# The second MLP of a window attention and two-MLP kernel in three tiles of 768 tokens, each product 384 columns wide

## The chip, the cores and the metric

The program runs on one core of a Trainium2 chip. The metric is the device time of one execution in microseconds (us). Before the change three runs gave 883.8, 884.16 and 888.37 us, so the median is 884.16 us.

## The reference

Attention over a window of 64 positions (4 batches, 8 heads, 576 positions, head size 64) gives 2304 tokens of 512 features. Two MLPs follow, each 512 to 2048 to 512, all in float32:

```python
def _moe_ref(x, w_in, w_out):
    h = x @ w_in
    r = np.maximum(h, 0.0)
    g = r * r
    return (g @ w_out).astype(np.float32)

def _moe2_ref(x, w_in, w_out):
    h = x @ w_in
    g = np.maximum(h, 0.0) + np.log1p(np.exp(-np.abs(h)))
    return (g @ w_out).astype(np.float32)
...
    x = _moe_ref(x=x, **moe_kwargs)
    return _moe2_ref(x=x, **moe2_kwargs)
```

## The kernel before

**Products.** Every operand of an MLP is split into a high and a low part in a format that TensorE reads in one pass, and every product is three matmuls: high by high, low weights by high, high weights by low. The first product of an MLP (x by w_in) is done with seven products of half-size matrices in place of eight (the names A, B, C, T1, T2, T3, T4 stand for the seven). The sums of weights that this needs are prepared once (`add_weights`, `add_sums`) on VectorE (DVE) and ScalarE (ACT), stored to DRAM (`d_in`, `d_out`), and streamed back through the rings `ri` and `ro`; the sums of inputs are made by `add_mats` for each tile.

**Second MLP.** There are four tiles of 512 tokens and one of 256. A tile has eight blocks; `add_block` makes two chunks of 128 hidden features: 7 products of 6 matmuls with 256 columns. `PA` puts A and T2 side by side into one PSUM bank (`pa`), `PB` puts T3 and T1 into another (`pb`), ACT copies `pa` to `wk` (`EA`), DVE adds (`U2`, `UB`), then `PC` puts B and C into `pa`, `PD` puts T4 into `pb`, and DVE makes the two chunks (`CC`, `CD`). Four banks may hold such products (class `h2`), so two blocks can be in flight; the four others hold the sums of the second product (class `acc`). The tile of 256 tokens uses plain products (`l1_small`, 12 matmuls of 256 columns for a chunk). `add_smooth` then works on each chunk: ACT does Abs, Exp, +1 and Ln, DVE three operations; `add_split` gives `gh` (ACT) and `gl` (DVE). `add_l2` is the second product, job `K`: for each 128 tokens 3 matmuls of 512 columns into `acc`.

**Order.** A planner (class `Plan`) writes all engines' instructions out in one fixed order before launch: jobs wait for others, take slots of pools (`caps`), and run by a rank, which is a due time shifted by the table `SHIFT`. On the chip each engine runs its list strictly in that order. All DMAs are issued by SyncE (SP) in that order too. Preparing the second MLP's weights is interleaved with the first MLP and with the beginning of the second.

Names in instruction rows: `pa1_2_7` is the bank `pa` of the second MLP (1), tile 2, block 7; a number behind it is the buffer's. `gh1_3_2` is MLP 1, tile 3, chunk 2. `halvesw...` and `area` are buffers that were something else before.

Of the kernel before, what the change touches and what calls it, by code (L numbers as in the profile page):

```python
# [1387 lines left out]
```

## Time and profile before

| | us |
|---|---|
| median of three runs | 884.16 |
| the profiled execution | 885.8 |
| its span, first to last instruction | 884.0 |
| TensorE busy in the span | 861.9 |
| VectorE, ScalarE busy | 742.0, 597.2 |

The profiled execution took 1.8 us more than its span and lies 1.6 us above the median. TensorE's busy time is made from modelled ends of pipelined matmuls, so a busy TensorE may still be at less than its full rate; how far apart matmuls start tells the rate. The first MLP and attention take the span to about 500 us, the second MLP the rest; the two overlap around there.

### The profile page before, as it was taken

How to read it: one execution, taken by the hardware profiler on the slowest of the kernel's cores; microseconds unless marked ns; L12 is line 12 of the kernel's file. 1: busy time of each engine (PE TensorE's matmuls, PEld its weight loads, DVE VectorE, ACT ScalarE, POOL GpSimd, SP SyncE). 2: the span in 40 equal slices, each digit the busy share in tenths (PEclk: the TensorE clock that was granted, in tenths of full speed). 3: DMA queues.
4: the chain of work that ended last, by engine and by line, in shares of the span. 5: the costliest groups of instructions: out<-in, count | busy, mean ns of one | idle time of the engine just before them, and what ended most of it. 6: DMA issues, size and time to landing. Idle time of an engine off the chain costs nothing.

```text
span 884.0 us, 17073 instructions
## 1 busy us (share of the span) xinstructions
PE 861.9 (98%) x6220; PEld 783.1 (89%) x6220; DVE 742.0 (84%) x1404; ACT 597.2 (68%) x1266; POOL 3.6 (0%) x19
## 2 busy tenths in 40 slices
PE   7799999999999999999999999999999999999998
PEld 6599999999898889888899988888898989899897
DVE  6899999899999999599655999998779667877754
ACT  5777776577675776466445867868568667766765
POOL 1000000000000000000000000000000000000000
PEclk9899999999999999999999999999999999999999
DMA  9999987999999999999999999899936872788581
GB/s 203 315 288 364 308 307 235 297 322 301 338 288 371 278 315 333 312 350 315 331 346 349 342 340 367 327 324 335 325 124 198 298 256 66 265 276 276 181 294 49
DMA packets 169987, 254.35 MB, mean 288 GB/s; under 512 B 65584, under 2 KB 119856, under 8 KB 169904
## 3 DMA queue, kind: packets, MB, share of 16 engines
q1 hardware_dynamic: 169904, 253.27, 87.0%
q8 instruction: 49, 0.80, 0.4%
q14 instruction: 34, 0.28, 0.1%
HBM read 193.46 MB, written 59.77 MB: 286 GB/s over the span
## 4 chain that ended last, share of the span: by engine, by line
PE 76%; DVE 10%; SPq 5%; DMA 3%; ACT 3%; issue 2%; DVEq 0%; ACTq 0%
PE acc L826 38%; PE pa L998 5%; PE pa L1001 5%; PE pa L999 4%; PE pb L998 4%; PE pb L1001 3%; PE pb L999 3%; SPq L607 2%; PE h L799 2%; PE h L800 2%; PE h L802 2%; SPq L440 2%; PE sc L646 1%; PE po L709 1%; DVE gl L847 1%
## 5 line engine op out<-in xcount | busy, mean ns | idle before, releaser
L826 PE MATMUL acc<-ro,gh 128*128 128x512 f32 x576 | 178.8, 392 | 0.0
L826 PE MATMUL acc<-gh,ro 128*128 128x512 f32 x384 | 121.9, 399 | 0.5 <-ACT gh L844 0.5
L826 PEld LDWEIGHTS acc<-ro,gh 128*128 128x128 f32 x576 | 104.3, 189 | 18.6
L826 PE MATMUL acc<-ro,gl 128*128 128x512 f32 x288 | 112.1, 389 | 0.0
L1101 DVE SCALAR_TENSOR_TENSOR e<-u,e 128x512 f32<-128x512 f32 (+1 forms) x80 | 50.8, 635 | 56.4 <-ACT u L1095 56.3
L998 PE MATMUL pb<-xT,ri 128*128 128x256 f32 x336 | 89.0, 287 | 3.1 <-DVE wk L1030 1.8
L999 PE MATMUL pb<-xT,ri 128*128 128x256 f32 x336 | 87.8, 283 | 0.0
L826 PEld LDWEIGHTS acc<-gh,ro 128*128 128x128 f32 x384 | 69.7, 190 | 14.0 <-issue 0.7
L826 PE MATMUL acc<-gl,ro 128*128 128x512 f32 x192 | 75.6, 394 | 0.3 <-DVE gl L847 0.3
L844 ACT CAST gh<-l 128x512 fp32r<-128x512 f32 (+1 forms) x80 | 45.7, 572 | 44.3 <-DVE l L1105 29.5
L998 PEld LDWEIGHTS pb<-xT,ri 128*128 128x128 f32 x336 | 64.1, 191 | 5.7 <-DVE wk L1030 2.0
L1001 PE MATMUL pb<-xT,ri 128*128 128x256 f32 x336 | 67.8, 283 | 0.1
L826 PE MATMUL acc<-gh,w 128*128 128x384 f32 x256 | 66.0, 338 | 0.0
L999 PEld LDWEIGHTS pb<-xT,ri 128*128 128x128 f32 x336 | 64.3, 191 | 1.2
L826 PEld LDWEIGHTS acc<-ro,gl 128*128 128x128 f32 x288 | 54.1, 188 | 12.0 <-DVE gl L847 0.3
L847 DVE TENSOR_TENSOR gl<-l,gh 128x512 fp32r<-128x512 f32 (+1 forms) x80 | 50.4, 630 | 4.0 <-ACT gh L844 3.6
L1001 PEld LDWEIGHTS pb<-xT,ri 128*128 128x128 f32 x336 | 52.4, 192 | 0.3 <-DVE xT L971 0.3
L1105 DVE TENSOR_TENSOR l<-l,e 128x512 f32<-128x512 f32 (+1 forms) x80 | 50.6, 632 | 2.3
L1093 ACT ACTIVATE e<-c 128x512 f32<-128x512 f32 (+1 forms) x53 | 29.5, 556 | 31.2 <-DVE c L1035 11.9
L1096 ACT ACTIVATE l<-u 128x512 f32<-128x512 f32 (+1 forms) x80 | 47.2, 590 | 2.6
L1094 ACT ACTIVATE e<-e 128x512 f32<-128x512 f32 (+1 forms) x80 | 47.2, 590 | 2.5
L1095 ACT ACTIVATE u<-e 128x512 f32<-128x512 f32 (+1 forms) x80 | 47.2, 589 | 2.5
(226 smaller groups left out, 2298.6 us busy)
## 6 DMA issues: line engine op xcount, KB each, us to landing
ri<-di SPq DMA_DIRECT2D x154, 512.0 KB, 6.2
ro<-do SPq DMA_DIRECT2D x92, 512.0 KB, 6.2
ri<-di SPq DMA_DIRECT2D x46, 256.0 KB, 5.4
raw<-in_moe_w_in_dram SPq DMA_DIRECT2D x16, 512.0 KB, 8.8
raw<-in_moe_w_out_dram SPq DMA_DIRECT2D x16, 512.0 KB, 6.7
di<-w SPq DMA_DIRECT2D x32, 256.0 KB, 4.8
do<-w SPq DMA_DIRECT2D x16, 512.0 KB, 5.7
di<-osa SPq DMA_DIRECT2D x32, 256.0 KB, 5.4
```

The lines of the kernel that those rows point to most:

```text
L826: nc.tensor.matmul(o, lh, rh, start=st and i == 0, stop=sp and i == 2)
L844: nc.scalar.copy(out=place(j, f"gh{me}", [P, T], F32R), in_=live[src])
L847: nc.vector.tensor_tensor(out=place(j, f"gl{me}", [P, T], F32R), in0=live[src], in1=f32(live[f"gh{me}"]), op=ALU.subtract)
L998: nc.tensor.matmul(out, w[:, 0, c, :], x[:, 0, c, :], start=(c == 0), stop=False)
L999: nc.tensor.matmul(out, w[:, 1, c, :], x[:, 0, c, :], start=False, stop=False)
L1001: nc.tensor.matmul(out, w[:, 0, c, :], x[:, 1, c, :], start=False, stop=(c == 1))
L1093: nc.scalar.activation(out=e, in_=live[src], func=AF.Abs)
L1094: nc.scalar.activation(out=e, in_=e, func=AF.Exp, scale=-1.0)
L1095: nc.scalar.add(u, e, 1.0)
L1096: nc.scalar.activation(out=g, in_=u, func=AF.Ln)
L1101: nc.vector.scalar_tensor_tensor(out=e, in0=u, scalar=1.0, in1=e, op0=ALU.subtract, op1=ALU.subtract)
L1105: nc.vector.tensor_tensor(out=live[f"l{me}"], in0=live[f"l{me}"], in1=live[f"e{me}"], op=ALU.add)
```

## The change

The second MLP's tokens are cut into three tiles of 768, each half 384 tokens, so each of the seven products is 6 matmuls of 384 columns and fills a bank alone (384 of its 512 columns). `add_block2` takes the place of `add_block` there. A (`PA`) goes into a fresh bank `pa`, T2 (`PC`), T3 (`PE`) and T4 (`PF`) are added on to it in the bank; between them ACT copies the running sum out (`EA`, `EB`, `EC`, and `ED` on ACT or DVE). B (`PB`) fills `pb`, which DVE adds to the first copy (`CA`); T1 (`PD`) fills `pd`, DVE takes a sum (`CB`), C (`PG`) is added on, and DVE takes another (`CD`). So three banks are used in turn but only two may be held at a time (`h2` is 2, it was 4); six hold the sums of the second product (`acc2`), which now comes in pieces of 3 times 128 tokens, 9 matmuls of 512 columns (`add_l2_half`, four pieces for a block). Activation works on pieces of 384 columns; its +1 may run on ACT or DVE. In the second MLP the rings have 7 and 5 slots (10 and 8 in the first). One of the eight stored weight matrices of a pair of chunks is no longer stored, and the tile of 256 tokens with `l1_small` is gone. The intermediate result is stored in pieces cut at 384 and read back in quarters (`add_quarter`). All values of `SHIFT` are new, and with them the order everywhere, first MLP included; the table below is cut to its first lines.

```diff
-    "p0": 29.16, "p1": 55.79, "p2": 8.83, "p3": 78.04, "p4": 42.73, "p5": -9.29, "p6": 11.94, "p7": 21.26,
...
+    "p0": 47.73, "p1": 20.45, "p2": -4.33, "p3": 0.75, "p4": -9.19, "p5": -12.85, "p6": -29.59, "p7": -15.58,
...
-    TILES = ((384, 384, 512, 512, 512), (512, 512, 512, 512, 256))
+    TILES = ((384, 384, 512, 512, 512), (768, 768, 768))
...
+    R = 3 * P
+    NRI2, NRO2 = 7, 5
...
-            "acc": 4, "h": 2, "h2": 4, "att0": 6, "att": 2, "s1": 4, "stash1": 8, "g1": 2, "pro1": 16,
-            "z0": 3, "zr": 2, "z1": 3, "zs": 2, "cc": 4, "tmp": 3, "y": 4, "st": 2,
+            "acc": 4, "acc2": 6, "h": 2, "h2": 2, "att0": 6, "att": 2, "s1": 4, "stash1": 8, "g1": 2, "pro1": 16,
+            "z0": 3, "zr": 2, "z1": 3, "zs": 2, "cc": 4, "cc2": 7, "tmp": 3, "y": 4, "st": 2, "st2": 4, "tmp2": 2,
...
-        (ph, b): dpool.tile([P, 8, 2, Q], F32, tag=f"di{ph}_{b}", name=f"di{ph}_{b}") for ph in range(2) for b in range(NB)
+        (ph, b): dpool.tile([P, 7, 2, Q], F32, tag=f"di{ph}_{b}", name=f"di{ph}_{b}") for ph in range(2) for b in range(NB)
...
-                put_mats(f // 2, ph, 0, 7, t)
+
+                nc.sync.dma_start(out=d_in[ph, f // 2][:, MAT[ph]["T4"]], in_=f32(t[:, :, Q:]))
...
+    def add_l2_half(t, f, h, begins, ends, ready, at, give, w_of):
+
+        me = f"1_{t}_{f}_{h}"
+        cs = range(3 * h, 3 * h + 3)
+
+        def fn(j):
+            a, b = live[f"gh{me}"], live[f"gl{me}"]
+            w = w_of()
+            for c in cs:
+                if begins:
+                    place(j, f"acc1_{t}_{c}", [P, DM], F32)
+                s = slice((c - 3 * h) * P, (c - 3 * h + 1) * P)
+                o = live[f"acc1_{t}_{c}"]
+                for k, (lh, rh) in enumerate(((a[:, s], w[:, 0, :]), (a[:, s], w[:, 1, :]), (b[:, s], w[:, 0, :]))):
+                    nc.tensor.matmul(o, lh, rh, start=begins and k == 0, stop=ends and k == 2)
+
...
+        ONE = 1.05
+        add(f"PA{me}", {"PE": ONE}, first("pa", "A"), [f"L{units[0]}", x_keys["A"]], at, bank("pa"), give_x[0], lag=0.25, then=chain["pb"])
+        add(f"EA{me}", {"ACT": 0.44}, out_a(0), [f"PA{me}"], take=[("wk", None, 1, [f"wk{me}"])])
+        add(f"PB{me}", {"PE": ONE}, first("pb", "B"), [f"PA{me}", f"L{units[1]}", x_keys["B"]], at + 1.05, bank("pb"), give_x[1], lag=0.25)
+        add(f"CA{me}", {"DVE": 0.47}, sum_of(0, 0, "pb", 0), [f"PB{me}", f"EA{me}"], take=piece(0, 0), give=[f"pb{me}"])
+        add(f"PC{me}", {"PE": ONE}, onto("pa", "T2"), [f"EA{me}", f"PB{me}", x_keys["T2"]], at + 2.1, give=give_in[1] + give_x[2], lag=0.25)
+        add(f"EB{me}", {"ACT": 0.44}, out_a(1), [f"PC{me}"])
+        add(f"PD{me}", {"PE": ONE}, first("pd", "T1"), [f"PC{me}", f"CA{me}", x_keys["T1"]], at + 3.15, bank("pd"), give_in[0] + give_x[3], lag=0.25)
+        chain["pb"] = f"PD{me}"
+        add(f"PE{me}", {"PE": ONE}, onto("pa", "T3"), [f"EB{me}", f"PD{me}", f"L{units[2]}", x_keys["T3"]], at + 4.2, give=give_x[4], lag=0.25)
+        add(f"EC{me}", {"ACT": 0.44}, out_a(2), [f"PE{me}"])
+        add(f"CB{me}", {"DVE": 0.47}, sum_of(1, 1, "pd", 2), [f"PD{me}", f"EC{me}"], take=piece(1, 1))
+        add(f"PF{me}", {"PE": ONE}, onto("pa", "T4"), [f"EC{me}", x_keys["T4"]], at + 5.25, give=give_in[2] + give_x[5], lag=0.25)
+        add(f"ED{me}", {"ACT": 0.44, "DVE": 0.47}, last_a, [f"PF{me}"], take=piece(1, 0), give=[f"pa{me}"])
+        add(f"PG{me}", {"PE": ONE}, onto("pd", "C"), [f"CB{me}", f"L{units[3]}", x_keys["C"]], at + 6.3, give=give_in[3] + give_x[6], lag=0.25)
+        add(f"CD{me}", {"DVE": 0.47}, sum_of(0, 1, "pd", 1), [f"PG{me}"], take=piece(0, 1), give=[f"pd{me}", f"wk{me}"])
+        return f"CA{me}", f"CB{me}", f"ED{me}", f"CD{me}"
...
+        def smooth_1(j):
+            e, _, _ = (place(j, f"{n}{me}", [P, T], F32) for n in "eul")
             nc.scalar.activation(out=e, in_=live[src], func=AF.Abs)
+
+        def smooth_2(j):
+            e = live[f"e{me}"]
             nc.scalar.activation(out=e, in_=e, func=AF.Exp, scale=-1.0)
-            nc.scalar.add(u, e, 1.0)
-            nc.scalar.activation(out=g, in_=u, func=AF.Ln)
+
+        def smooth_3(j):
+            if j.who == "ACT":
+                nc.scalar.add(live[f"u{me}"], live[f"e{me}"], 1.0)
+            else:
+                nc.vector.tensor_scalar_add(live[f"u{me}"], live[f"e{me}"], 1.0)
+
+        def smooth_4(j):
+            nc.scalar.activation(out=live[f"l{me}"], in_=live[f"u{me}"], func=AF.Ln)
...
+            for o, (k, h) in enumerate(((0, 0), (1, 1), (1, 0), (0, 1))):
+                f = 2 * b + k
+                add_smooth(t, f, h, sums[o])
+                begins, ends = i == 0 and o < 2, i == NB - 1 and o > 1
+                key = add_l2_half(
+                    t, f, h, begins, ends, [f"L{outs[n][k]}"], at + 1.3 * BLOCK2 + 2.1 * o, give_outs[n][k] if o > 1 else [],
+                    lambda w=outs[n][k]: live[w],
                 )
-        if i == NB - 1:
-            (add_result1 if ph == 0 else add_result2)(t, key, at + 2.2 * BLOCK)
+                if ends:
+                    add_result2(t, h, key, at + 2.2 * BLOCK2)
```

**First place.** TensorE (PE) in the second MLP, behind a piece of second product, before; tile 3, block 0.

```order
L998 MATMUL pa1_3_0_9962<-xC1_3_9110,ri55_2_9776 128x256
L999 MATMUL pa1_3_0_9962<-xC1_3_9110,ri55_2_9776 128x256
L998 MATMUL pa1_3_0_9962<-xC1_3_9110,ri55_2_9776 128x256
L999 MATMUL pa1_3_0_9962<-xC1_3_9110,ri55_2_9776 128x256
L1001 MATMUL pa1_3_0_9962<-xC1_3_9110,ri55_2_9776 128x256 x2
L826 MATMUL acc1_3_0_9370<-ro54_0_9616,gh1_3_2_10002 128x512 x2
L826 MATMUL acc1_3_0_9370<-ro54_0_9616,gl1_3_2_10008 128x512
L826 MATMUL acc1_3_1_9371<-ro54_0_9616,gh1_3_2_10002 128x512 x2
```

And after the change, the last tile's last block.

```order
L1027 MATMUL pb1_2_7_10119<-xB1_2_8829,ri47_1_9915 128x384 x6
L1027 MATMUL pa1_2_7_10079<-hxT21_2_8859,ri47_1_9915 128x384 x4
L1027 MATMUL pa1_2_7_10079<-lxT21_2_8860,ri47_1_9915 128x384 x2
L1027 MATMUL pd1_2_7_10142<-hxT11_2_8882,ri47_0_9843 128x384 x4
L1027 MATMUL pd1_2_7_10142<-lxT11_2_8883,ri47_0_9843 128x384 x2
L1027 MATMUL pa1_2_7_10079<-hxT31_2_8918,ri47_2_9945 128x384 x4
L1027 MATMUL pa1_2_7_10079<-lxT31_2_8919,ri47_2_9945 128x384 x2
L848 MATMUL acc1_2_0_9093<-ro46_1_9876,gh1_2_13_0_10110 128x512 x2
```

Before, a product is 6 matmuls of 256 columns, and C fills the second half of `pa`; now B, T2, T1 and T3 follow each other with 6 matmuls of 384 columns each, T3 onto the bank that T2 has just left.

**Second place.** ACT where the second MLP begins, before: behind the split of the first MLP's chunk 14.

```order
L844 CAST gh0_4_14_6237<-c0_4_14_6214 128x512
L464 ACTIVATE halvesw1_15_2726<-area_76 128x512
L1093 ACTIVATE e1_0_0_6257<-halvesw1_15_2726 128x512
L1094 ACTIVATE e1_0_0_6257<-e1_0_0_6257 128x512
L1095 ACTIVATE u1_0_0_6258<-e1_0_0_6257 128x512
L1096 ACTIVATE l1_0_0_6259<-u1_0_0_6258 128x512
L490 CAST area_76<-z1_9_1_6216 128x512
L1079 ACTIVATE c0_4_15_6292<-c0_4_15_6292 128x512
L405 COPY wk1_0_1_6311<-pa1_0_1_6279 128x512
L844 CAST gh0_4_15_6317<-c0_4_15_6292 128x512
```

After, from the activation of the second MLP's first piece on.

```order
L1192 ACTIVATE e1_0_0_0_6205<-c1_0_0_0_6186 128x384
L1177 ACTIVATE c0_4_15_6203<-c0_4_15_6203 128x512
L1196 ACTIVATE e1_0_0_0_6205<-e1_0_0_0_6205 128x384
L879 ACTIVATE c0_4_15_6203<-c0_4_15_6203 128x512
L1200 ACTIVATE u1_0_0_0_6206<-e1_0_0_0_6205 128x384
L864 CAST gh0_4_15_6224<-c0_4_15_6203 128x512
L1205 ACTIVATE l1_0_0_0_6207<-u1_0_0_0_6206 128x384
L1131 COPY wk1_0_0_6152<-pa1_0_0_6127 128x384
L1000 CAST hxC1_0_6241<-st1_0_11_5306 128x768
L487 CAST area_76<-z1_6_1_6122 128x512
L1131 COPY wk1_0_0_6152<-pa1_0_0_6127 128x384
```

The copy of T2's sum, the first `wk1_0_0` row, now stands behind the chain of activations of two chunks, and a second copy of the same block three rows later.

**Third place.** ACT at the end of the program, before: the last three chunks, each 256 columns.

```order
L1094 ACTIVATE e1_4_14_10638<-e1_4_14_10638 128x256
L1095 ACTIVATE u1_4_14_10639<-e1_4_14_10638 128x256
L1096 ACTIVATE l1_4_14_10640<-u1_4_14_10639 128x256
L844 CAST gh1_4_13_10658<-l1_4_13_10607 128x256
L1093 ACTIVATE e1_4_15_10671<-c1_4_15_10645 128x256
L1094 ACTIVATE e1_4_15_10671<-e1_4_15_10671 128x256
L1095 ACTIVATE u1_4_15_10672<-e1_4_15_10671 128x256
L1096 ACTIVATE l1_4_15_10673<-u1_4_15_10672 128x256
L844 CAST gh1_4_14_10684<-l1_4_14_10640 128x256
L844 CAST gh1_4_15_10697<-l1_4_15_10673 128x256
```

After: the last two pieces, each 384 columns.

```order
L397 COPY c1_2_15_0_10217<-pa1_2_7_10079 128x384
L864 CAST gh1_2_15_1_10219<-l1_2_15_1_10181 128x384
L1192 ACTIVATE e1_2_15_0_10221<-c1_2_15_0_10217 128x384
L1196 ACTIVATE e1_2_15_0_10221<-e1_2_15_0_10221 128x384
L1200 ACTIVATE u1_2_15_0_10222<-e1_2_15_0_10221 128x384
L1205 ACTIVATE l1_2_15_0_10223<-u1_2_15_0_10222 128x384
L1192 ACTIVATE e1_2_14_1_10248<-halvesw1_15_2742 128x384
L1196 ACTIVATE e1_2_14_1_10248<-e1_2_14_1_10248 128x384
L1200 ACTIVATE u1_2_14_1_10249<-e1_2_14_1_10248 128x384
L864 CAST gh1_2_15_0_10255<-l1_2_15_0_10223 128x384
L1205 ACTIVATE l1_2_14_1_10250<-u1_2_14_1_10249 128x384
L864 CAST gh1_2_14_1_10272<-l1_2_14_1_10250 128x384
```

The high part of the piece before the last (`gh1_2_15_0`) now stands behind three operations of the last piece (`1_2_14_1`).

## Rows read from the trace of the kernel before

**Rows 1.** Page, share of the span by engine; then the chain that ended last
```profile
PE 861.9 (98%) x6220; PEld 783.1 (89%) x6220; DVE 742.0 (84%) x1404; ACT 597.2 (68%) x1266; POOL 3.6 (0%) x19
...
PE 76%; DVE 10%; SPq 5%; DMA 3%; ACT 3%; issue 2%; DVEq 0%; ACTq 0%
```

**Rows 2.** Stretches of 50 us: busy us and instructions by engine, clock, DMA share, GB/s
```profile
500.00:550.00 50.00, 48.15 (x303) 43.39 (x302) 48.76 (x90) 38.74 (x67) 0.00 (x0) 1.00 1.01 352
550.00:600.00 50.00, 48.63 (x319) 44.05 (x318) 49.26 (x85) 37.76 (x66) 0.00 (x0) 1.00 0.93 336
600.00:650.00 50.00, 50.00 (x293) 44.43 (x292) 39.52 (x65) 34.65 (x59) 0.00 (x0) 1.00 0.81 282
```

**Rows 3.** TensorE in order of time: start us, us, what, how many in a run
```profile
58.87 0.33 PE L799 MATMUL h<-xh,w 128*128 128x384 f32 x1
...
60.95 0.33 PE L799 MATMUL h<-xh,w 128*128 128x384 f32 x1
...
610.29 0.61 PE L826 MATMUL acc<-ro,gh 128*128 128x512 f32 x2
...
610.97 0.61 PE L826 MATMUL acc<-ro,gh 128*128 128x512 f32 x2
...
621.85 0.28 PE L998 MATMUL pb<-xT,ri 128*128 128x256 f32 x1
...
622.57 0.28 PE L998 MATMUL pb<-xT,ri 128*128 128x256 f32 x1
```

**Rows 4.** Timeline, TensorE waits; in brackets idle us and releaser
```profile
398.58 0.39 PE L998 MATMUL pb<-xT,ri 128*128 128x256 f32 x1 [1.76 <-DVE wk L1030]
...
508.39 0.39 PE L998 MATMUL pa<-xB,ri 128*128 128x256 f32 x1 [0.49 <-ACT wk L405]
...
537.35 0.39 PE L998 MATMUL pa<-xB,ri 128*128 128x256 f32 x1 [1.37 <-ACT wk L405]
...
587.18 0.39 PE L998 MATMUL pb<-xT,ri 128*128 128x256 f32 x1 [1.16 <-DVE c L1041]
```

**Rows 5.** Short stretches behind two of these waits, columns as in Rows 2
```profile
400.00:401.00 1.00, 1.00 (x4) 0.81 (x4) 1.00 (x3) 0.64 (x2) 0.00 (x0) 0.50 1.09 384
...
538.00:540.00 2.00, 2.00 (x14) 1.82 (x14) 2.00 (x5) 0.10 (x1) 0.00 (x0) 1.00 0.87 304
```

**Rows 6.** Timeline, a sum or copy between two matmuls
```profile
586.44 0.68 DVE L1041 TENSOR_TENSOR c<-pb,wk 128x512 f32<-128x512 f32 x1
...
874.03 0.64 PE L1142 MATMUL c<-xl,ri 128*128 128x256 f32 x4
...
874.71 0.38 ACT L1093 ACTIVATE e<-c 128x256 f32<-128x256 f32 x1 [0.79 <-PE c L1142]
```

**Rows 7.** Timeline, instructions that follow each other on one engine
```profile
121.76 0.48 ACT L869 ACTIVATE area<-h 128x384 f32<-128x384 f32 x1
122.27 0.53 ACT L859 ACTIVATE area<-area 128x384 f32<-128x384 f32 x1
...
135.45 0.55 DVE L405 COPY r<-acc 128x384 f32<-128x384 f32 x1
...
135.92 0.55 DVE L847 TENSOR_TENSOR gl<-area,gh 128x384 fp32r<-128x384 f32 x1
...
506.51 0.68 DVE L1105 TENSOR_TENSOR l<-l,e 128x512 f32<-128x512 f32 x1
...
507.11 0.68 DVE L483 SCALAR_TENSOR_TENSOR z<-area,z 128x512 uint32<-128x512 uint32 x1
```

**Rows 8.** Chain in order of time: start us, us, what, how many
```profile
382.31 0.34 DVE z L467
...
399.56 4.34 PE acc L826 x12
408.21 2.75 PE acc L826 x12
...
874.67 5.48 PE acc L826 x24
```

More of the change, by code (lines that the diff above doesn't have):

```diff
@@ L522, in add_weights @@
         add(
-            f"SW{me}", {"DMA": 1.52}, store, [last], give=[raw] if ph else [], rank=want, lag=4.0,
+            f"SW{me}", {"DMA": 1.52 if which or f % 2 == 0 else 0.78}, store, [last], give=[raw] if ph else [], rank=want, lag=4.0,
         )
@@ L784, in add_pair, with units_in @@
         return add(f"XL{p}", {"DVE": 0.61}, x_lo, [f"XH{p}"], give=[f"po{p}"])
-    gh, gl = {}, {}
-    yd = [dpool.tile([P, KC, Q], F32, tag=f"y{u}", name=f"yd{u}") for u in range(NT // Q)]
+    slots_of = {}
+    cuts = sorted({NT, *T0S[0], *range(0, NT, R)})
+    units_y = list(zip(cuts, cuts[1:]))
+    yd = {u: dpool.tile([P, KC, u[1] - u[0]], F32, tag=f"y{u[0]}", name=f"yd{u[0]}") for u in units_y}
+    def units_in(t0, t1):
+        return [u for u in units_y if t0 <= u[0] and u[1] <= t1]
     order2 = []
@@ L829, in add_l2 @@
         before = order2[-1] if n else None
         order2.append(key)
+        def fn(j):
+            a, b = live[f"gh0_{t}_{f}"], live[f"gl0_{t}_{f}"]
+            w = w_of(f)
+            for c in range(KC):
+                if n == 0:
+                    place(j, f"acc0_{t}_{c}", [P, DM], F32)
+                s = slice(c * P, (c + 1) * P)
+                o = live[f"acc0_{t}_{c}"][:, 0:T]
+                for k, (lh, rh) in enumerate(((w[:, 0, s], a), (w[:, 1, s], a), (w[:, 0, s], b))):
+                    nc.tensor.matmul(o, lh, rh, start=n == 0 and k == 0, stop=n == NF - 1 and k == 2)
@@ L831, in add_l2 @@
         return add(
[L832 to L841 removed]
+            key, {"PE": {384: 2.09, 512: 2.78}[T]}, fn, [f"Gl0_{t}_{f}", *ready, before], at,
@@ L843, in g_hi, with add_split @@
+    def add_split(me, T, src, after):
+        cost = {384: (0.44, 0.48), 512: (0.54, 0.6)}[T]
         def g_hi(j):
@@ L1168, in store @@
             return fn
-        for c in range(TILES[1][t] // P):
+        for c in range(3 * half, 3 * half + 3):
             add(
@@ L1278, in window_attention_moe_moe2 @@
             at += step * NB
+    N_USES1 = sum(u[0] == 0 for u in uses)
     def rings(kind, n_ring, wants):
@@ L1320, in window_attention_moe_moe2 @@
             add_ring_out(name, *w, at - 15.0)
[L1321 to L1330 removed]
+        x_names = [slots_of[f"x{m}{ph}_{t}"] if i == NB - 1 else [] for m in MATS[ph]]
```

321 lines of the change are left out of this document (166 added, 155 removed), and 96 rows, old and new, of the table SHIFT.

## The prediction

> **What bounds the kernel now.** I read the page first. TensorE is busy for 98% of the span and the chain that ended last runs on it for 76% [rows 1], so the question is how much time TensorE's own list takes and how long it stands. The timeline answers the first: matmuls start 0.72 us per 6 at 256 columns (0.120 us each), 2.08 us per 12 at 384 (0.173 us), 0.68 us per 3 at 512 (0.227 us) [rows 3]. That is columns at 2.4 GHz plus 0.013 us for each matmul. Second, its waits: in the second MLP three longer ones, 0.49, 1.37 and 1.16 us, each ended by a copy or sum that empties a product's bank [rows 4]. All three lie before 600 us, where VectorE is busy for 48.8 and 49.3 of 50 us; behind it TensorE shows 50.00 of 50 us with VectorE at 39.5 [rows 2]. The second MLP is therefore bound by TensorE's list, and in its first 100 us also by VectorE, which has the weights' preparation to do beside the blocks.
>
> **What is taken away.** First products before: 4 tiles x 8 blocks x 7 products x 6 = 1344 matmuls, and 16 chunks x 12 = 192 for the small tile, 1536 in all of 256 columns, 1536 x 0.120 = 184.3 us. After: 3 x 8 x 7 x 6 = 1008 of 384 columns, 1008 x 0.1733 = 174.7 us. The second products stay 18 token groups x 16 chunks x 3 = 864 matmuls x 0.227 = 195.8 us. So TensorE's list gets **9.6 us** shorter: 7.0 us for 528 matmuls fewer at 0.013 us, 2.6 us for columns, since the small tile did without the seven-product form. No tail hides this: TensorE issues without a gap in both lists.
>
> The Trainium skill ("TensorE: Matmul & The Clock Gate", Back-to-back issue gap) gives columns / 2.4 plus 2.5 ns for a lone stream; by it the sum would be 1536 x 0.109 minus 1008 x 0.163, so 3.9 us in place of 9.6. This case's rows differ from it at all three widths (0.120, 0.173, 0.227 us), so the measured number decides.
>
> The three waits of rows 4 that lie in the second MLP, **3.0 us**, sit in blocks that no longer exist; I count them as gone, and count new ones by themselves.
>
> **What is added: handing a bank over.** Before, four banks were there for products and a copy had at least the next bank's two products to hide behind. After, T2, T3 and T4 are added on in the bank from which ACT must first have copied, T1 waits for the sum over B, the next block's A and B for the last copies: seven handovers a block, 166 in all with the last block's two left out. One costs: the tail of the last matmul, 0.33 - 0.17 = 0.16 us [rows 3]; 0.04 us until the reader starts (874.03 + 0.64 to 874.71 [rows 6]); the copy, 0.48 us on ACT or 0.55 on DVE at 384 columns [rows 7]; and 0.06 us back to TensorE (586.44 + 0.68 = 587.12, TensorE at 587.18 [rows 4, 6]). That is 0.74 or 0.81 us, if the reader is free. I went through TensorE's list after the change: 129 handovers have two or more products or a piece of second product (2.04 us) in between. 37 have a single product, 1.04 us: 15 from T2 to T3, 13 from B to T1, 6 from T4 to the next A, 2 from C to the next B, 1 from A to T2; the first place of the change shows two of them. They have 0.2 to 0.3 us to spare, half an instruction of the reader. What stands behind a late one is all of TensorE's list.
>
> Where VectorE has room that is enough. From tile 2 on, a block takes 15.4 us on TensorE (42 x 0.173 + 36 x 0.227) and 19 full and 2 short operations of 384 columns on VectorE, 19 x 0.47 + 2 x 0.27 = 9.5 us or 61% (0.47 is the distance of the DVE rows, 135.45 to 135.92 [rows 7]; 0.27 an estimate: the short one's 0.34 at 512 columns [rows 8] less a half of 0.13, the step between 384 and 512). I take nothing there; the cover is VectorE's 39% of free time.
>
> Where it has none: between the `gl` of the second MLP's first piece and that of chunk 15's, VectorE's list holds 142 operations of 384 columns, 42 of 512 at 0.60 [rows 7], 22 short ones of 512 at 0.34, 11 of 768, 8 of 256 and 7 short ones of 384. With 768 and 256 columns estimated by the step of 0.13 (0.86, 0.34) that is 66.7 + 25.2 + 7.5 + 9.5 + 2.7 + 1.9 = 113.5 us. TensorE's list in the same stretch is 29 pieces x 2.04 + 51 products x 1.04 = 112.2 us. VectorE was about 98% busy in such a stretch [rows 2], so it needs 113.5 / 0.98 = 115.8 us, and TensorE stands for **3.6 us**. Bounds: 0, if work runs ahead as far as the list allows; 14, if each of the 14 single-product handovers of tile 0 costs the mean of the three known waits, 1.0 us.
>
> **Beginning of the second MLP.** The copy of T2's sum stands on ACT behind seven other instructions (second place), which start with the activation of B's sum. At some 0.5 us each [rows 7] from B's end + 2.2 us on (VectorE has two operations of 0.6 and 0.9 us in front of that sum), the copy ends about **0.9 us** after T3 could start. Bounds 0 and 2.
>
> **End.** Now the program's last piece waits for its activation. Count from the end of the last product, C. Its sum is there after 0.8 us, then Abs, Exp and +1 take 1.5 us on ACT; only behind them stands `gh` of the piece before (third place), so its second product starts at 2.9 in place of 2.0 us. VectorE then does that piece's `gl` and three operations for the last one (to 4.9 us), ACT its `gh` (5.4), VectorE its `gl` (6.0): the last piece ends at 7.6 us where TensorE's list alone would end at 6.1, so **1.5 us** more. Before, the last 24 matmuls run in 5.48 us, as the rate of rows 3 has it, and wait for nothing [rows 8]. Bounds 0 and 3.
>
> **Rest.** First MLP and attention: the same instructions in another order. Up to 500 us there is a wait of 1.76 us (398.58 [rows 4]) and the half clock behind it, in which 12 matmuls took 4.34 us and not 2.75 [rows 8], 3.4 us in all, which a new order may save or double: 0, bounds -4 and +4. Ring loads fall from 200 and 92 to 168 and 76 in the order; no wait of TensorE in the second MLP ends on a DMA [rows 4], so I count nothing for them.
>
> **Sum.** -9.6 - 3.0 + 3.6 + 0.9 + 1.5 = -6.6 us. On the profiled execution's 885.8 us that is 879.2; it lies 1.6 us above the median, so for a median of runs 884.16 - 6.6 = **877.5 us**. No change can be told from one of 0.5%, 4.4 us.
>
> **Rivals.**
> *All of it comes through* (no new waits, and the 3.4 us of the first MLP are saved too): 884.2 - 9.6 - 3.0, less up to 3.4, 868 to 872 us. For it speaks that after 600 us nothing waits now; against it VectorE's 113.5 us against 112.2.
> *The waits eat it* (10 to 15 us of new ones in place of 6): 882 to 887 us, no change. For it, the 0.2 us to spare.
> *Slower: VectorE's list runs late in the stretch full of preparation, so that every single-product handover of tile 0 is late.* 14 x 1.0 us; and such waits can add up to a lowered clock: behind the wait of 1.76 us the granted clock was 0.50 (1.2 GHz), behind 1.37 us it stayed 1.00 (2.4 GHz) [rows 4, 5], at 1.6 us a time. With two to four of these: -9.6 - 3.0 + 14 + 2.4 + 3.2 to 6.4 = +7 to +10, 891 to 894 us. It decides the sign when tile 0's 14 handovers wait more than 0.7 us on average. Against it: before, only three of the many handovers in a stretch as full were late.
> The Trainium skill ("Perfetto Trace Analysis", Optimizing Tensor Performance, Matmuls) asks for independent groups to rotate through the PSUM banks, so that emptying one overlaps the next, which speaks for this rival; the free 0.2 us are what the rows leave of that overlap.
> *Only the columns count*: if the 0.013 us of a matmul are not saved with its number but grow with the wider operand, the list shrinks by the columns alone, 6144 / 2.4 GHz = 2.6 us, and with the waits above it is 884.2 - 2.6 + 3.0 = 884.6 us, no change. Rows 3 speak against it: 384 columns cost the same 0.013 us as 256. The rule of the Trainium skill that is weighed above (Back-to-back issue gap) goes the same way.
>
> **Chances.** The forecast, 874 to 881 us, 0.46; all comes through 0.20; eaten 0.16; slower 0.15; only the columns 0.03. The border for faster is 879.7 us, which leaves about 0.10 of the forecast's 0.46 in "same": faster 0.36 + 0.20 = 0.56, same 0.10 + 0.16 + 0.03 = 0.29, slower 0.15. The range goes from the middle of the full gain to the top of "same": 870 to 888 us.
>
> **What would show it.** Matmuls of the products 0.173 us apart; no waits of TensorE in tile 2 but at its end; in tile 0 waits of single products, 0.3 to 1.4 us, ended by `wk` or DVE sums, 2 to 6 us in all, with VectorE near 98%; about 1.5 us of waits in the last 8 us. I am wrong if single products wait in tiles 1 and 2 as well (then the handover costs more than 0.8 us), if the clock is at 0.50 anywhere past 450 us, or if the first MLP's end has moved by more than 4 us.

## The result and the profile after

The changed kernel takes 875.03 us (median of 4 runs, 873.95 to 875.71) beside 883.98 us of the kernel before (4 runs, 883.57 to 888.37): a ratio of 0.9876, 95% interval 0.9846 to 0.9907, 9.0 us. The forecast was 877.5 us. Its profiled execution has a span of 873.9 us beside 884.0, so the trace has 10.1 us to account for, 1.1 more than the medians: the profiled execution of the kernel before (885.8 us) lies 1.8 us above its median, that of the changed kernel (875.71 us) 0.7 us above.

Busy time by engine and the chain that ended last, on the page of the changed kernel:

```profile
PE 852.3 (98%) x5692; PEld 771.0 (88%) x5692; DVE 723.1 (83%) x1427; ACT 614.1 (70%) x1375; POOL 3.6 (0%) x19
...
PE 86%; DVE 5%; DMA 4%; SPq 3%; ACT 1%; issue 1%; DVEq 0%; ACTq 0%
```

528 matmuls fewer, as counted; TensorE's part of the chain is up from 76% [rows 1]. The products' pitch in its timeline (start, duration, matmuls in a group) is the one expected:

```profile
849.05 0.85 PE L1027 MATMUL pa<-hxT,ri 128*128 128x384 f32 x4
849.74 0.51 PE L1027 MATMUL pa<-lxT,ri 128*128 128x384 f32 x2
850.09 0.85 PE L1027 MATMUL pd<-hxT,ri 128*128 128x384 f32 x4
850.78 0.51 PE L1027 MATMUL pd<-lxT,ri 128*128 128x384 f32 x2
851.13 0.85 PE L1027 MATMUL pa<-hxT,ri 128*128 128x384 f32 x4
```

849.05 to 850.09 to 851.13: 1.04 us for 6 matmuls of 384 columns, 0.173 each. These rows are also T2, T1 and T3 of one block: T3 goes onto T2's bank with a single product between, and TensorE does not stand. In windows of 50 us, to be set beside [rows 2]:

```profile
500.00:550.00 50.00, 49.26 (x243) 43.47 (x242) 49.45 (x102) 43.88 (x92) 0.00 (x0) 1.00 0.95 324
550.00:600.00 50.00, 49.38 (x247) 43.90 (x246) 49.12 (x99) 40.27 (x84) 0.00 (x0) 1.00 0.84 300
600.00:650.00 50.00, 50.00 (x246) 44.45 (x245) 40.19 (x74) 37.95 (x79) 0.00 (x0) 1.00 0.58 186
```

VectorE is as full as before up to 600 us, TensorE a little fuller. TensorE's waits from 480 to 600 us (in total, times, longest), then from 850 us on:

```profile
PE pa L1027 <- ACT c L397: 0.7, 2, 0.5
PE pa L1027 <- ACT wk L1131: 0.5, 1, 0.5
PE pd L1027 <- DVE c L1139: 0.5, 1, 0.5
...
PE acc L848 <- ACT gh L864: 1.3, 2, 0.9
```

They replace the 3.0 us of [rows 4] by 1.7 us, all at single products, and add the pair at the end.

Waits are not all. The table takes, for each matmul, the time to the next one's start less its pitch of [rows 3], summed by stretch ("lost"); the first column has the time before the first matmul in it. Pitches by themselves sum to 849.2 us before and 839.6 after. Labels other than "before" and "changed" are those of the experiments below; VectorE's busy time is from the windows view. Values below zero are the formula's error at the attention's matmuls of 64 and 128 columns, many of which start 7 ns behind the one before.

| kernel | to 60 us | 60-250 | 250-480 | 480-600 | 600-850 | from 850 | last start to end | VectorE busy 250-480 |
|---|---|---|---|---|---|---|---|---|
| before | 19.9 | -0.9 | 5.3 | 5.2 | 1.2 | 0.2 | 4.2 | 188 |
| before, again (e8) | 19.1 | -1.8 | 6.6 | 5.7 | 1.2 | 0.2 | 4.2 | 188 |
| e2 | 18.3 | -1.3 | 4.4 | 35.2 | 2.4 | 0.3 | 4.2 | 178 |
| e11 | 18.3 | -1.2 | 6.2 | 13.8 | 1.4 | 0.2 | 4.2 | 195 |
| **changed** | 18.3 | -0.9 | 0.4 | 5.7 | 3.5 | 2.4 | 5.3 | 180 |
| e1 | 19.0 | 1.1 | 0.7 | 4.2 | 4.0 | 2.4 | 4.9 | 185 |
| e10 | 19.9 | 1.1 | 0.6 | 16.7 | 7.7 | 2.6 | 5.5 | 183 |
| e9 | 18.3 | -1.3 | 0.2 | 26.1 | 6.2 | 2.7 | 5.2 | 175 |
| e7 | 18.2 | 7.3 | 3.7 | 4.0 | 3.7 | 2.5 | 4.8 | 188 |
| e4 | 18.5 | -1.3 | 1.2 | 2.9 | 3.5 | 2.4 | 5.3 | 176 |
| e5 | 17.9 | -1.2 | 0.4 | 6.1 | 6.9 | 2.7 | 5.3 | 180 |
| e6 | 17.4 | -1.4 | 0.2 | 5.1 | 3.5 | 2.0 | 4.6 | 181 |
| e12 | 18.3 | -1.2 | 0.3 | 4.6 | 3.5 | 0.7 | 4.9 | 181 |

Changed less before: -9.6 (pitches), -1.6, 0.0, -4.9, +0.5, +2.3, +2.2, +1.1, together -10.0 of the 10.1 us.

### The profile page after: what moved, and what is told of

It reads as the page before. It is cut to its first block, busy times and chain, and to the rows that moved or that the text cites. A ratio compares the mean times of both kernels' runs of the same rounds, so it can differ in the third digit from the quotient of the medians.

```text
span 873.9 us, 16020 instructions
## 1 busy us (share of the span) xinstructions
PE 852.3 (98%) x5692; PEld 771.0 (88%) x5692; DVE 723.1 (83%) x1427; ACT 614.1 (70%) x1375; POOL 3.6 (0%) x19
## 4 chain that ended last, share of the span: by engine, by line
PE 86%; DVE 5%; DMA 4%; SPq 3%; ACT 1%; issue 1%; DVEq 0%; ACTq 0%
PE acc L826 22%; PE acc L848 20%; PE pa L1027 17%; PE pb L1027 8%; PE pd L1027 5%; PE h L804 3%; PE h L805 3%; PE h L807 3%; SPq L606 2%; PE po L708 2%; PE sc L645 2%; PE pp L689 2%; DMA area<-in_moe_w_out_dram 1%; DMA k<-in_k_dram 1%; DMA area<-in_moe_w_in_dram 1%
## 5 line engine op out<-in xcount | busy, mean ns | idle before, releaser
L867 DVE TENSOR_TENSOR gl<-l,gh 128x384 fp32r<-128x384 f32 x96 | 53.3, 556 | 17.9 <-ACT gh L864 16.2
L1210 DVE SCALAR_TENSOR_TENSOR e<-u,e 128x384 f32<-128x384 f32 x96 | 53.1, 553 | 14.8 <-ACT u L1200 14.8
L1027 PE MATMUL pa<-hxT,ri 128*128 128x384 f32 x288 | 62.2, 337 | 0.5 <-ACT wk L1131 0.5
L1027 PE MATMUL pb<-xT,ri 128*128 128x256 f32 x432 | 60.5, 285 | 0.0
L1027 PEld LDWEIGHTS pb<-xT,ri 128*128 128x128 f32 x432 | 56.1, 191 | 1.7 <-DMA area<-in_moe_w_in_dram 0.2
L1214 DVE TENSOR_TENSOR l<-l,e 128x384 f32<-128x384 f32 x96 | 53.2, 554 | 4.2
L1027 PEld LDWEIGHTS pa<-hxT,ri 128*128 128x128 f32 x288 | 51.5, 188 | 3.4 <-ACT wk L1131 1.1
L1205 ACT ACTIVATE l<-u 128x384 f32<-128x384 f32 x96 | 50.4, 525 | 3.5 <-DVE u L1202 2.0
L1027 PE MATMUL pa<-xA,ri 128*128 128x256 f32 (+1 forms) x288 | 51.2, 313 | 0.7 <-ACT c L397 0.7
L1196 ACT ACTIVATE e<-e 128x384 f32<-128x384 f32 x96 | 50.5, 526 | 2.0
```

The lines of the kernel that those rows point to most:

```text
L867: nc.vector.tensor_tensor(out=place(j, f"gl{me}", [P, T], F32R), in0=live[src], in1=f32(live[f"gh{me}"]), op=ALU.subtract)
L1027: nc.tensor.matmul(out, w[:, s, c, :], x[k][:, c, :], start=(i == 0 and not on), stop=(i == 5), skip_group_check=on)
L1196: nc.scalar.activation(out=e, in_=e, func=AF.Exp, scale=-1.0)
L1205: nc.scalar.activation(out=live[f"l{me}"], in_=live[f"u{me}"], func=AF.Ln)
L1210: nc.vector.scalar_tensor_tensor(out=e, in0=u, scalar=1.0, in1=e, op0=ALU.subtract, op1=ALU.subtract)
L1214: nc.vector.tensor_tensor(out=live[f"l{me}"], in0=live[f"l{me}"], in1=live[f"e{me}"], op=ALU.add)
```

## The experiments

**e4, less work for VectorE.** In the preparation of the weights that come last:

```diff
+        few = ph == 1 and ORDER.index((f, which)) >= 19
+
         def hold(j):
+            if few:
+                return
```

and the same return in shift and top.

> The changed kernel without three of VectorE's five preparation steps (the clamp, the shift and the upper word) for the last 13 of the second MLP's 32 weight tiles: 13 x 1.28 = 16.6 us of VectorE's work out of the stretch up to 600 us, where it is 98% busy; those weights are no longer the reference's. Theory, TensorE's waits between 480 and 600 us (about 3 us) come from VectorE being full: they fall to 1 us or less, and the time to about 872.5 us, 871.5 to 873.5. Rival, a single product of 1.04 us is too little cover for a handover as such: the waits stay, 875 us.

873.21 us (ratio to before 0.9864, 0.9818 to 0.9910), 1.8 us below the changed kernel, with intervals that overlap; the trace has the place. Of the waits from 480 to 600 us one is left:

```profile
PE pa L1035 <- ACT wk L1139: 0.3, 1, 0.3
```

Lost time there falls from 5.7 to 2.9 us (5.1 and 4.6 in e6 and e12, which do not touch this stretch), the span by 2.1. Of the 1.7 us of waits in tile 0, 1.4 are VectorE's load: a single product is cover enough in all places but one. The 2.9 us that stay are partly the same kind of place, 0.2 to 0.6 us at four of them, and partly spread over all matmuls.

**e5, a dearer handover.**

```diff
-                nc.scalar.copy(out=live[f"wk{me}"][:, i], in_=live[f"pa{me}"])
+                for _ in range(2 if i == 1 else 1):
+                    nc.scalar.copy(out=live[f"wk{me}"][:, i], in_=live[f"pa{me}"])
```

> The changed kernel with ScalarE's copy of T2's sum made twice in every block of the second MLP (24 copies more). Where ScalarE is free, the changed kernel's trace has 0.37 us from the last matmul to the copy, 0.48 us for the copy and 0.36 us more until T3 starts, of which 0.05 us are needed: 0.31 us to spare where a single product lies between, which is so in 15 of 24 blocks. Theory, a handover is hidden as long as copy and cover are in that proportion and not longer: with 0.5 us more each of the 11 free ones is late by 0.2 us, and the four beside a busy ScalarE by up to 0.5: 2 to 4 us more, 877 to 879 us, with waits of TensorE on that copy from 600 to 850 us, where there are none now. Rival, the room is larger than it looks, since the work between can move: 875 us. Other rival, ScalarE's later work is pushed back too: above 881 us.

879.36 us (0.9943, 0.9924 to 0.9963), 0.4 us above the theory's 877 to 879. T1 (`pd`), the copy of T2's sum and T3 (`pa`), in the timeline of the changed kernel and then, one block later, of this one:

```profile
834.45 0.85 PE L1027 MATMUL pd<-hxT,ri 128*128 128x384 f32 x4
...
834.65 0.48 ACT L1131 COPY wk<-pa 128x384 f32<-128x384 f32 x1
...
835.49 0.85 PE L1027 MATMUL pa<-hxT,ri 128*128 128x384 f32 x4
```

```profile
853.41 0.85 PE L1027 MATMUL pd<-hxT,ri 128*128 128x384 f32 x4
853.61 0.99 ACT L1132 COPY wk<-pa 128x384 f32<-128x384 f32 x2
...
854.66 0.97 PE L1027 MATMUL pa<-hxT,ri 128*128 128x384 f32 x4
```

T1 to T3 is 1.04 us with one copy. With two, T3 starts 0.06 us behind the second, 1.25 us behind T1, and its first four take 0.97 in place of 0.85: 0.3 us a place. Lost time from 600 to 850 us goes from 3.5 to 6.9. The waits view prints none of it, since each wait is short, so a sum over starts is needed to see it.

**e3, the products in halves.**

```diff
+            if me_x[0] == "1":
+                for g in (slice(0, 192), slice(192, 384)):
+                    nc.tensor.matmul(
+                        out[:, g], w[:, s, c, :], x[k][:, c, g], start=(i == 0 and not on), stop=(i == 5),
...
```

The products' sums are then not the reference's; only the time is read.

> The changed kernel with each matmul of the second MLP's products issued as two of 192 columns: the same columns, 1008 matmuls more. Theory, each matmul costs 0.013 us beyond its columns: starts 0.0933 us apart, 1008 x 0.0133 = 13.4 us more, 888.4 us (887 to 890). Rival, only columns count: 875 us, starts 0.087 us apart. If the weight load of 128 columns has become the limit, starts are further apart than 0.0933 us and the time is above 890.

917.83 us (1.0374, 1.0313 to 1.0436), the third case. Ten matmuls of 192 columns in a row:

```profile
887.94 1.26 PE L1029 MATMUL pb<-xB,ri 128*128 128x192 f32 x10
```

(1.26 - 0.27) / 9 = 0.110 us, neither 0.0933 nor 0.087, so columns and a fixed part are not told apart this way; weight loads start 0.112 us apart there. That the load sets the spacing is argued from this agreement, not shown by a run of its own. The Trainium skill ("TensorE: Matmul & The Clock Gate", LDWEIGHTS) gives a weight load as its columns / 1.2 in ns, an estimate of 107 ns for 128 columns; the measured 112 ns is 5% above it. The question itself is answered by the pitch of 0.173 us above.

**e6 and e12, the end.** e6 gives the first piece of the last block one dependency more:

```diff
                 key = add_l2_half(
-                    t, f, h, begins, ends, [f"L{outs[n][k]}"],
+                    t, f, h, begins, ends, [f"L{outs[n][k]}", "PG1_2_7" if (t, i, o) == (2, NB - 1, 0) else None],
...
```

> The changed kernel with one dependency more: in the last block the second product's third-last-but-one piece (K of chunk 14, first half) goes behind the last product C, in place of ahead of it. TensorE then has 4 x 2.04 us behind C in place of 3 x 2.04. Theory, the two waits at the end (1.05 and 0.59 us) are the last pieces' activations, 5.9 us behind C against 4.1 us of cover: both go, 1.6 us less, 873.4 us, and C itself does not wait since the piece of chunk 12 still lies between. Rival, the activations move back by the same time: 875.0 us, with the same waits.

873.92 us (0.9875, 0.9847 to 0.9902): 1.1 us lower, with intervals that overlap, and not for the reason given. The two waits of 0.88 and 0.43 us are one of 1.49 us now, so the waiting stays, as the rival had it (timelines of the changed kernel, then of e6):

```profile
863.63 0.73 PE L848 MATMUL acc<-ro,gh 128*128 128x512 f32 x2 [0.88 <-ACT gh L864]
...
866.54 0.73 PE L848 MATMUL acc<-ro,gh 128*128 128x512 f32 x2 [0.43 <-ACT gh L864]
```

```profile
860.82 1.02 DVE L1214 TENSOR_TENSOR l<-l,e 128x384 f32<-128x384 f32 x2
...
861.46 0.98 ACT L864 CAST gh<-l 128x384 fp32r<-128x384 f32 x2 [2.12 <-DVE l L1214]
...
862.03 0.73 PE L848 MATMUL acc<-ro,gh 128*128 128x512 f32 x2 [1.49 <-ACT gh L864]
```

ScalarE and VectorE had worked on the last two activations in turns, so that the first was as late as the second: the last sum (`l`) and the high part (`gh`) of both stand back to back. The span is 3.1 us shorter than the changed kernel's, but only 1.1 of that lies from 850 us on; the rest is in stretches that the edit does not touch. e12 keeps e6's edit and puts them one behind the other:

```diff
+        end = (t, f, h) == (2, 14, 1)
...
-        add(f"Sx{me}", {"ACT": act}, smooth_2, [f"Sw{me}"])
+        add(f"Sx{me}", {"ACT": act}, smooth_2, [f"Sw{me}", "Sa1_2_15_0" if end else None])
...
-        add(f"Sb{me}", {"DVE": 2 * dve}, smooth_b, [f"Sa{me}"], give=[src, f"u{me}"], lag=0.0)
+        add(f"Sb{me}", {"DVE": 2 * dve}, smooth_b, [f"Sa{me}", "Sc1_2_15_0" if end else None], give=[src, f"u{me}"], lag=0.0)
```

> The changed kernel with a second-product piece more behind the last product C, as in the run on the end, and with the last two activations one behind the other: the last piece's Exp waits for the Ln of the piece before, its first multiply for that piece's last sum. In that run ScalarE and VectorE had done the two in turns, so that both came 5.8 us behind C, and the wait was 1.65 us as before (1.05 + 0.59). Theory, one behind the other the first is there some 4.4 us behind C and the last 6 us: 0.7 us of waits are left, 1 us less, 874 us. Rival, what is left of the chain on VectorE (gl of the one behind two multiplies of the other) holds it: waits of 1.4 us or more, 875 us.

873.08 us (0.9865, 0.9835 to 0.9896). One wait is left in its timeline:

```profile
861.91 0.50 PE L848 MATMUL acc<-ro,gl 128*128 128x512 f32 x1 [0.16 <-DVE gl L867]
```

Lost time from 850 us on is 0.7 us in place of 2.4, as the theory had it. Its median is 2.0 us below the changed kernel's, with intervals that overlap; the trace shows 1.7 us of it where the edit is. It has the lowest median of the runs that compute the whole result, though not clear of the changed kernel's.

**e1 and e2, the first half's order.** My first theory on the 6.5 us gained ahead of 480 us: the new table of numbers. e1 is the changed kernel with 168 of the old numbers, e2 the kernel before with 168 of the new ones (the diffs of the table here and below are e1's and e7's, with lines cut short):

```diff
-    "p0": 47.73, "p1": 20.45,
+    "p0": 29.16, "p1": 55.79,
...
-    "R4": 64.86,
+    "R4": 143.61,
```

> The changed kernel, but with the numbers of the kernel before in the order's table for everything that belongs to the attention, the first MLP's weights and the first MLP (168 of 288 numbers). Theory: the order of the first half, which the new table sets, saved about 6.7 us there, and the second MLP gave the rest; so TensorE's losses before 480 us come back to about 20 us (13.5 with the new table), and the time is 875.0 + 6.7 = 881.7 us, 878 to 884. Rival 1, the difference of the first half is luck of the profiled runs: 875 us, within 1.5. Rival 2, it comes from the other edits that reach the first half (smaller stores of the prepared weights, seven matrices of a block in place of eight): 875 us too, with TensorE's losses before 480 us as in the changed kernel.

> The kernel before, but with the new table's 168 numbers for the attention and the first MLP; its second MLP stays in tiles of 512 tokens. Theory (the table's order saved the first half's time): 884.0 - 6.7 = 877.3 us, 875 to 881, with TensorE's losses before 480 us near 14 us in place of 23. The second MLP's numbers are the old ones and fit the new first half less well, which may give 1 to 3 us back. Rivals 1 and 2 of the run above: 884 us, within 1.5.

e1 took 875.78 us (0.9897, 0.9863 to 0.9932), e2 913.88 us (1.0330, 1.0290 to 1.0369). The theory fell: of 6.5 us e1 loses 3.0 again up to 480 us and has 1.4 back behind it, so its median is not to be told from the changed kernel's; e2 loses 35 us in the second MLP's first tile, where the old numbers for the weights' preparation no longer fit (with these renewed too, e11 loses 13.8 there). What holds is that the first 60 us go with the table: 19.0 to 19.9 us under the old numbers (before, e8, e1, e10), 17.4 to 18.5 under the new ones (all others).

**e7 and e9, the second MLP's weights.** e7 lowers the 24 numbers of their preparation (16 W1, 8 S1) by 30 us, e9 takes the old ones (its expectation says 40, and those of e10 and e11 say 208 in place of 192):

```diff
-    "W1_0_0": 16.45, "S1_0": -12.58, "W1_1_0": 35.32,
+    "W1_0_0": -13.55, "S1_0": -42.58, "W1_1_0": 5.32,
```

> The changed kernel with 30 us taken off the table's numbers for the preparation of the second MLP's weights: in the order 4 of the 32 weight tiles in place of 8 are prepared by VectorE behind the second MLP's first activation, so 4 x 2.5 = 10 us of its work move to the time before 480 us, where it is busy for 63 to 75% between 400 and 500 us. Theory (VectorE is what makes the waits of tile 0): TensorE's losses from 480 to 600 us fall from 5.7 to 3 to 4 us, 872.5 to 873.5 us. Rival, VectorE is as full from 100 to 400 us, and the work moved there makes new waits of the first MLP and the attention: losses before 480 us rise by as much or more, 875 us or above.

> The changed kernel with the old table's 40 numbers for the preparation of the second MLP's weights (W1 and S1) alone. Runs so far: with the old numbers for attention and first MLP but the new ones for this preparation, TensorE lost 0.7 us between 250 and 480 us, like the changed kernel (0.4); with it the other way round 4.4, like the kernel before (5.3). Theory, where this preparation falls among VectorE's work sets the waits of 250 to 480 us: about 4 us of losses come back there, 879 us, 877.5 to 881. Rival, they come from old preparation and old attention together: 875 to 876 us.

e7: 886.05 us (1.0017, 0.9998 to 1.0035). Tile 0 gains as the theory said (5.7 to 4.0, beside 4.6 in e12 without such an edit), but the first MLP and the attention lose 11.5 us: the rival. Its longest wait between 250 and 480 us, 2.1 us, ends on a load into the ring `ri`. e9: 896.88 us (1.0137, 1.0105 to 1.0168), both of my cases missed. Up to 480 us it is like the changed kernel; the weights come too late for tile 0 (TensorE's waits, 480 to 620 us):

```profile
PE acc L846 <- DMA ro<-do: 7.8, 1, 7.8
PE acc L846 <- ACT halvesw L459: 4.2, 1, 4.2
```

**e10 and e11, all numbers ahead of the second MLP exchanged.** 192 numbers, the 168 and the 24, edited as in e1 and e2.

> The changed kernel with all of the old table's numbers for what runs ahead of the second MLP: attention, both MLPs' weights, first MLP (208 numbers); only the second MLP's own numbers are new. Theory, the order of the first half (the table, not the second MLP's tiles) gave 6 to 7 us of the 9: TensorE's first start and losses up to 480 us come to 23 to 25 us as in the kernel before (17.7 in the changed one), 880 to 883 us. Rival, the smaller stores, the seven matrices of a block and the rings have a part in it: losses up to 480 us stay below 21 us, 878 us or less.

> The kernel before with the new table's 208 numbers for all that runs ahead of the second MLP, its own tiles of 512 tokens kept. Theory, the order of the first half is worth its 6 to 7 us without the change of tiles: losses and first start up to 480 us at 17 to 19 us, and the losses of the second MLP's beginning (35 us, when only the preparation was left old) back at 5 to 8 us: 877 to 880 us. Rival, the first half's new order lives on the new second MLP (room and rings given up earlier): losses up to 480 us above 21 us, or over 10 us lost behind 480 us: 884 us or more.

895.80 us (1.0123, 1.0078 to 1.0169) and 893.86 us (1.0105, 1.0074 to 1.0137). e10 missed both of its cases: up to 480 us it loses 21.6 us, between the theory's 23 and the rival's 21, and the time is far above both, for the 16.7 us of tile 0. e11 is its rival: 23.3 us up to 480 us and 13.8 in tile 0. In the column of 250 to 480 us the kernel before has 4.4 to 6.6 us under three tables (before, e2, e11), and the changed one 0.2 to 0.7 under four (its own, e1, e9, e10). That part does not come with the table alone. But it is not one loss that stays with the kernel before. The longest waits there have other places and other releasers under each table (timelines of before, e2 and e11; the one at 398 us is in [rows 4]):

```profile
274.23 0.63 PE L690 MATMUL pp<-ident,k 128*128 128x128 f32 x4 [0.73 <-ACT q L671]
...
288.99 0.73 PE L826 MATMUL acc<-gh,ro 128*128 128x512 f32 x2 [0.47 <-ACT gh L844]
```

```profile
253.29 0.63 PE L614 MATMUL tk<-ident,k 128*128 128x128 f32 x4 [1.95 <-DMA k<-in_k_dram]
```

```profile
262.63 0.63 PE L614 MATMUL tq<-ident,q 128*128 128x128 f32 x4 [1.21 <-DMA q<-in_q_dram]
...
413.37 0.39 PE L994 MATMUL pa<-xB,ri 128*128 128x256 f32 x1 [2.27 <-ACT wk L401]
```

**e8, the kernel before again.**

> The kernel before once more, for a second profile. Theory, its times from 880.7 to 888.0 us differ by stretches of half clock (3.4 us long, so 1.7 us each) behind waits of the first 400 us, which come and go from one execution to the next: this profile has other waits there than the first (0.5 us or more of difference in the first 60 us or at 274, 289 or 398 us), each half clock less goes with 1.7 us less, and the second MLP's waits (0.49, 1.37, 1.16 us) come back within 0.3 us. Rival, the waits of the first half are set by the order alone and come back as they were: 1.76 us at 398 us, half clock behind it, losses before 480 us of 24 us.

885.92 us, one run. The rival, mostly: the wait at 398 us is back (2.03 us from start to start beyond the pitch, 1.92 the first time) with half clock behind it, and so are those at 274 and 289 us and the three of the second MLP. The start differs: a wait for q of 2.2 us at 16.5 us, of 2.3 us at 20.7 the first time, and two stretches of half clock in the first 60 us in place of three. The theory's price for one stretch, 1.7 us, is not seen in the time (885.92 beside 885.8 us).

## Why the prediction held, step by step

- **Shorter list, -9.6 us:** right. The 9.6 is the count at the pitches of [rows 3], and the rows above show the 0.173 us at the new place; what matmuls took beyond their pitch stands under tile 2 below. *Only the columns count* is out.
- **Price of a handover:** right. Predicted 0.74 us behind the end of a product's columns and 0.2 to 0.3 to spare; with a free reader it is 0.37 us from the last matmul's start to the copy, 0.48 for it and 0.05 back, 0.90 in all or 0.73 without that matmul's own 0.17, and 0.31 to spare. e5 shows where that ends. *Slower* needed more than 0.7 us at each of tile 0's 14 single products; all losses of 480 to 600 us together are 5.7.
- **VectorE's full stretch and the beginning, +3.6 and +0.9, for -3.0 that go:** +1.5 net, measured +0.5. e4 shows VectorE's load as the cause of half of the 5.7 us lost in this stretch, and of 1.4 of the 1.7 us of waits. At the beginning the place was right (T3 behind the copy of T2, 0.49 us of wait, 0.66 lost).
- **No waits from tile 2 on:** none in the waits view, but 3.5 us are lost from 600 to 850 us, 2.3 more than before. They are spread over 1240 matmuls, about 3 ns each (before 0.8): at 512 columns the median is 0.230 us from start to start in place of 0.227. No single place has more than 0.11. Not foreseen and not explained.
- **End, +1.5:** 1.05 + 0.59 us lost at the two waits, 2.2 more than before in the stretch. I had put it on the order of ScalarE, behind whose three operations a `gh` stood; e6 and e12 show that it is the order of both engines' operations of the last two pieces, and that it can go with the two edits together. The 1.1 us more from the last matmul's start to the end was not counted.
- **"First MLP and attention: the same instructions in another order ... 0, bounds -4 and +4":** this step failed. It is -6.5 us, outside its own bounds, and one of the prediction's own signs of being wrong came true: the first MLP's end moved by more than 4 us. The last activation of the first MLP starts 7.6 us earlier (timelines of before, then of the changed kernel):

```profile
493.23 0.63 ACT L1079 ACTIVATE c<-c 128x512 f32<-128x512 f32 x1 [0.18 <-DVE c L1041]
```

```profile
485.65 0.62 ACT L1177 ACTIVATE c<-c 128x512 f32<-128x512 f32 x1
```

  The total came within 2.5 us because the tail and the fine losses, 3.4 us that I had not counted, stand against it. That is luck: two misses of opposite sign. The chance of 0.20 for *all comes through* was the nearest to this part, too small in what it allowed.

What made the 6.5 us: 1.6 in the first 60 us, with the table (e1 and e10 19.0 and 19.9, e2 and e11 18.3), of which 0.8 is what two executions of the kernel before differ by (19.9, and 19.1 in e8). 4.9 between 250 and 480 us, where the changed kernel is without the waits at 274, 289 and 398 us. There VectorE does 188 us of work before and 180 after, in one window each of the two traces (columns as in [rows 2]):

```profile
250.00:480.00 230.00, 226.69 (x1752) 202.82 (x1745) 188.44 (x359) 137.29 (x303) 0.00 (x0) 0.99 0.98 325
```

```profile
250.00:480.00 230.00, 229.62 (x1736) 207.02 (x1735) 180.36 (x339) 139.55 (x292) 0.00 (x0) 1.00 0.96 323
```

The lines view of VectorE from 250 to 480 us says what the 8 us are (one step of the weights' preparation, before, then changed):

```profile
L477 DVE SCALAR_TENSOR_TENSOR z<-area,z 128x512 uint32<-128x512 uint32 x14 | 9.6, 685 | 0.1
...
L477 DVE SCALAR_TENSOR_TENSOR halvesw<-area,halvesw 128x512 uint32<-128x512 uint32 x4 | 2.8, 688 | 0.1
```

```profile
L474 DVE SCALAR_TENSOR_TENSOR z<-area,z 128x512 uint32<-128x512 uint32 x12 | 8.3, 692 | 0.1
...
L474 DVE SCALAR_TENSOR_TENSOR halvesw<-area,halvesw 128x512 uint32<-128x512 uint32 x4 | 2.8, 696 | 0.1
```

18 weight tiles are prepared there before and 16 after, and the attention's row maxima are 12 before and 10 after; over the whole program both kernels have 64 and 36. So this work falls into other stretches; it is not taken off VectorE. In the other runs, e7, which moves the preparation forward, has 188 again and 3.7 us lost, 2.1 of them in a wait for a DMA; e2 with 178 and 4.4 does not fit. That less work of VectorE in this stretch is what frees it is my reading, not shown; which edit does it (smaller stores, fewer matrices, other rings) was not tried alone, and the cause stays open. Shown is that this preparation has a narrow place: earlier costs the first MLP and the attention 11.5 us (e7), later costs tile 0 over 20 us (e9).

## What to carry to other kernels

Where TensorE's list is the bound, count its matmuls times their pitch first: fewer, wider matmuls gave the 9.6 us of the count. A bank may be reused with one product between if reader and cover are counted (0.90 against 1.21 us from start to start) and the reader's engine has room; the room is the thing to check. And a forecast of a reordered program needs a term for the stretches whose instructions stay the same: here that term was the largest miss.

## What was not expected of the hardware

- **The clock behind waits.** In windows of 1 us the granted clock was 0.50 (1.2 GHz) in four stretches of the kernel before (about 21 to 24, 38 to 41, 45 to 48 and 399 to 403 us) and in one of the changed kernel (36 to 43 us), the end behind the last matmul left out. Rows of the kernel before, then of the changed one (the third number from the end is the clock; the last row is the place of [rows 5], now at full clock):

```profile
22.00:23.00 1.00, 1.00 (x26) 1.00 (x24) 0.93 (x4) 0.34 (x1) 0.00 (x0) 0.50 1.20 285
39.00:40.00 1.00, 1.00 (x4) 1.00 (x4) 0.97 (x3) 0.00 (x0) 0.00 (x0) 0.50 1.08 372
46.00:47.00 1.00, 1.00 (x4) 1.00 (x4) 1.00 (x3) 0.69 (x3) 0.00 (x0) 0.50 1.10 348
```

```profile
41.00:42.00 1.00, 1.00 (x10) 0.88 (x7) 0.78 (x2) 0.59 (x1) 0.00 (x0) 0.50 1.10 352
400.00:401.00 1.00, 1.00 (x6) 0.81 (x6) 1.00 (x4) 0.97 (x2) 0.00 (x0) 1.00 0.67 209
```

  One minus the clock, summed over the windows, is 6.8 us before and 3.4 after: up to 3.4 us of the gain. The length of a wait alone does not decide: 1.9 and 2.0 us at 398 us (before, e8) were followed by half clock, in e7 2.0 and 2.3 us at 217 and 273 us were not:

```profile
218.00:219.00 1.00, 0.93 (x5) 0.54 (x4) 0.99 (x3) 0.00 (x0) 0.00 (x0) 1.00 0.92 343
...
274.00:275.00 1.00, 1.00 (x8) 0.87 (x7) 0.90 (x2) 0.60 (x2) 0.00 (x0) 1.00 0.87 290
```
- **The spread of the kernel before goes with its clock.** Of 22 runs beside e5 to e7 (881.4 to 889.4 us) the six with a mean granted clock of 0.996 to 0.998 average 882.3 us, the four at 0.989 to 0.990 average 888.0. The changed kernel's four lie within 1.8 us.
- **A matmul behind a wait is slower:** the two behind the wait of 0.88 us took 0.73 us in place of 0.62, and that wait of 0.88 cost 1.05 from start to start. The first weight load starts with its matmul there (both at 863.63 us), not ahead of it; that this is where the 0.11 us go was not tried.
